# A new order for the opening of a linear-attention and gated-MLP kernel, with named PSUM banks and the first weight columns in four loads

## The chip, the cores and the metric

The kernel runs on one NeuronCore of one Trainium2 chip. The metric is the device time of one execution in microseconds (us). Before the change it is 321.68 us, the median of three runs (321.1 to 321.99). The profiled execution took 320.37 us, of which the profile's span covers 318.6 us.

The engines are named as in the profile: PE is the matrix engine (TensorE), PEld its weight loads, DVE is VectorE, ACT is ScalarE, POOL is GpSimd, SP is the engine that here only issues transfers. PSUM, which takes the matrix engine's results, has eight banks, numbered 0 to 7.

## The reference

Two steps in float32: a linear attention with a normalisation per head, then a gated MLP with a gated residual. Eight batches of 576 tokens, eight heads of 64, so 4608 tokens of 512 channels; the hidden width is 1536.

```python
kv  = einsum('bhsd,bhse->bhde', k, v)
o   = einsum('bhsd,bhde->bhse', q, kv)
x   = o / sqrt(mean(o * o, axis=-1) + 1e-6) * g_norm      # then (4608, 512)
g   = x @ w_gate
ffn = (0.5 * g * (1 + erf(g / sqrt(2))) * (x @ w_val)) @ w_out
out = x + ffn / (1 + exp(-(x @ w_res)))
```

## The kernel before

The tokens are worked in blocks of 512: of each batch the first 512 tokens are one block, in four tiles of 128 (`j`), and the 64 left over of all batches make a ninth block. Everything is computed in fp16 with fp32 sums. Block b's MLP runs on PE while the attention of batch b + 1 or b + 2 is worked beside it, so PE has work without a break, except in the opening: there batch 0 has no MLP beside it, and its attention must be through before the first MLP product.

The schedule is manual (`tc.manual_schedule()`, line 83): each engine executes its instructions in the order in which the program writes them. The opening's order is a string of words, `opening` (lines 1294 to 1299), read by `first_gval` and `f_piece`. A word names a step, then a pair of heads `pr` from 0 to 3 (128 channels), sometimes a half of the tiles (`a`, `b`), and in the last place an engine (`A`, `D`, `P`). An instruction that waits holds back what stands behind it on its own engine. For one pair the steps run as follows.

- `qc`, `kc`, `vc` cast the float32 arrivals of q, k and v to fp16. `lk` and `lv` put the last 64 tokens of k and v in place.
- `qT` transposes q on PE (four transposes), `qo` copies the result out of PSUM.
- `kv` multiplies k and v (six products), `kvo` (DVE) masks it into SBUF, `o` multiplies by q (four products).
- `sq` squares o (ACT), `rd` sums per head (DVE), `rt` is the root (ACT), `ri` the reciprocal (DVE), `t` the product o times reciprocal (DVE).
- `xT` transposes t (PE), and `xo` copies it out, scaled by the column `gcol` of g_norm.
- `g` and `v` are the products of that pair's 128 channels with the first 256 columns of w_gate and w_val, added up over the four pairs in four PSUM tiles (two of 128 columns for each weight).
- `warm` is a number of products of zeros, `keep_warm`, which nothing reads.

The first 256 columns of w_gate and w_val come as float32 through SP's queue, after all of q, k and v of batch 0 (line 1077), and are cast by the words `wcg` and `wcv` (half of the channels each). The other columns, `wg1` to `wg3` and `wv1` to `wv3` (256, 512 and 512 columns), are words too: POOL issues a transfer that casts on the way (`load_columns`, line 146). After the opening POOL issues in this order w_res (line 1600), batch 1 (`load_batch`, lines 120 to 122 and 109: q, k, v, then the last rows of k and of v), and w_out in four transfers (`load_wo`, line 1602: products 0 and 1, 2 and 3, 4 to 7, 8 to 11 of the hidden width).

PSUM tiles are taken from two rings of banks, `pmoe` and `pattn` (`Banks`, lines 61 to 75). A tile taken without a bank gets the ring's next one, so the bank follows from the order of the steps. A new tile in a bank must wait until the last reader of the tile before it is done.

After the opening come the MLP products of block 0: `m_gval(0, f)` for f from 2 to 7 (line 410, 8 products of 512 columns each), then a group of four by fewer products (line 946), the residual gate (line 430), the attention products of batch 1 (lines 187, 208), and then the products with w_out, one f after the other (line 447, `m_ffn`), with the second attention product of batch 1 (line 230) behind f = 0.

Of the kernel before, what the change touches and what calls it, by code (L numbers as in the profile page):

```python
# [8 lines left out]
FP32 = mybir.dt.float32  # L9
FP16 = mybir.dt.float16  # L10
# [8 lines left out]
def kernel(  # L19
# [15 lines left out]
    nc = tc.nc  # L35
    P = nc.NUM_PARTITIONS
    B, H, S, D = q.shape
    C = H * D
    F = moe_w_gate.shape[1]
    NP = H // 2  # L40
    NF = F // P
    NJ = 4
# [4 lines left out]
    WCS = (256, 256, 512, 512)  # L47
# [24 lines left out]
                self.turn.append(bank)  # L72
            return psum.tile(shape, dtype, tag=f"bank{bank}", name=name)

    pmoe, pattn = Banks(3, 1, 0, 2, opening=(0, 1, 2)), Banks(4, 5, 6, 7)

    def banks_behind():

# [55 lines left out]
    wg_c, wv_c = [], []  # L134
# [8 lines left out]
    th_all = finp.tile([P, NJ, C], FP32, bufs=1, name="th")  # L143
    res_all = finp.tile([P, NJ, C], FP32, bufs=1, name="osb")

    def load_columns(dst, src, i):
        c0 = sum(WCS[:i])
        nc.gpsimd.dma_start(out=dst[i], in_=src[:, c0 : c0 + WCS[i]].rearrange("(cc p) f -> p cc f", p=P))

    def load_wg(i):  # L150
        load_columns(wg_c, moe_w_gate, i)

    def load_wv(i):
        load_columns(wv_c, moe_w_val, i)

    def load_wo(f0, f1):
        nc.gpsimd.dma_start(
# [872 lines left out]
    for which in "kv":  # L1030
        if which == "k":
            t = hidp.tile([P, NF, NJ * P], FP16, tag="hid", name=which + "f").rearrange("p a b -> p (a b)")
        else:
            t = hid_s
# [8 lines left out]
    for which in "kv":  # L1043
        t = hid_of[which]
        rest = t[:, 2 * H * NJ * D :]
# [26 lines left out]
    w_raw = {}  # L1072
    for n, t in (("g", moe_w_gate), ("v", moe_w_val)):
        pool, tag = (stage, "qraw") if n == "g" else (qkvp, "k16")
        w_raw[n] = pool.tile([P, H, NJ * D], FP16, tag=tag, name=f"w{n}f")
        w_raw[n] = w_raw[n].rearrange("p a b -> p (a b)").bitcast(FP32).rearrange("p (c f) -> p c f", c=NP)
        nc.sync.dma_start(out=w_raw[n], in_=t[:, 0 : WCS[0]].rearrange("(cc p) f -> p cc f", p=P))
    ident32 = moep.tile([P, P], FP32, tag="ge", name="ident32")
    make_identity(nc, ident32)

# [10 lines left out]
    one32 = consts.tile([1, 1], FP32, name="one32")  # L1091
# [5 lines left out]
        out=of_head, in_=ident32.rearrange("p (r h) -> p h r", h=HH), op=ALU.add, axis=mybir.AxisListType.X  # L1097
    )
    grow32 = moep.tile([1, 2, D], FP32, tag="ge", name="grow32")
# [9 lines left out]
    def keep_warm(n):  # L1109
        for _ in range(n):  # L1110
            nc.tensor.matmul(idle, lhsT=zeros[:, 0:P], rhs=zeros, start=True, stop=True)  # L1111
# [5 lines left out]
    xT0, t0 = xT_t[0], t_t[0]  # L1117
    rms0 = consts.tile([P, NJ, H], FP32, name="rms0")
    rinv0 = consts.tile([P, NJ, H], FP32, name="rinv0")
    first = {}  # L1120
# [4 lines left out]
    def of_pair(pr):  # L1125
        return slice(2 * pr, 2 * pr + 2), slice(pr * P, (pr + 1) * P)

    def f_cast(which, pr, copy):
        hs, _ = of_pair(pr)
        dst, src = b16_t[0, which], raw[0, which]  # L1130
        if which == "v":
            copy(out=dst[:, hs, :], in_=src[:, hs, :])
        else:
            copy(
                out=dst.rearrange("p j h d -> p h j d")[:, hs, :, :],
                in_=src.rearrange("p h (j d) -> p h j d", j=NJ)[:, hs, :, :],
            )

    def f_k_last(half, engs):

        raw_ = first_raw[0][half].rearrange("p (j d) -> p j d", j=2)
        for j, eng in enumerate(engs):
            eng.tensor_tensor(
                out=first_last[0][:, j, half * HH : (half + 1) * HH, :],
                in0=raw_[:, j, None, :].to_broadcast([P, HH, D]),
                in1=of_head[:, :, None].to_broadcast([P, HH, D]),
                op=ALU.mult,
            )

    def f_v_last(half, copy):  # L1150
        raw_ = first_raw[1][half].rearrange("p (j d) -> p j d", j=2)
        copy(out=first_last[1][:, half], in_=raw_[:, :, None, :].to_broadcast([P, 2, 2, D]))

    def f_qT(pr):
        q16 = b16_t[0, "q"].rearrange("p j h d -> p j (h d)")
        first["qT", pr] = ps = pattn.tile([P, NJ, P], FP16, tag="at", name="qtp")
        for j in range(NJ):
            nc.tensor.transpose(ps[:, j, :], q16[:, j, of_pair(pr)[1]], ident)

# [2 lines left out]

    def f_kv(pr):

        first["kv", pr] = ps = pattn.tile([P, P], FP32, tag="at", name="kvp")
        k16 = b16_t[0, "k"].rearrange("p j h d -> p j (h d)")
        hs, cs = of_pair(pr)
        for j in range(NJ):
            nc.tensor.matmul(
                ps, lhsT=k16[:, j, cs], rhs=b16_t[0, "v"][:, hs, j * D : (j + 1) * D], start=(j == 0), stop=False  # L1170
            )
        for j in range(2):
            kl = first_last[0][:, j].rearrange("p h d -> p (h d)")[:, cs]
            vl = first_last[1][:, pr // 2, j].rearrange("p e d -> p (e d)")
            nc.tensor.matmul(ps, lhsT=kl, rhs=vl, start=False, stop=(j == 1))
# [2 lines left out]
        nc.vector.tensor_tensor(out=s0["kv2"][:, pr, :], in0=first["kv", pr], in1=mask, op=ALU.mult)  # L1178

    def f_o(pr):  # L1180
        pool, tag = (pmoe, "mm") if pr < 2 else (pattn, "at")
        first["o", pr] = ps = pool.tile([P, NJ, P], FP32, tag=tag, name="op")
        for j in range(NJ):
            nc.tensor.matmul(
                ps[:, j, :], lhsT=s0["qT"][:, j, pr, :], rhs=s0["kv2"][:, pr, :], start=True, stop=True
            )
# [27 lines left out]
        )  # L1214

    def f_xT(pr, j0, j1):
        first["xT", pr, j0] = ps = pattn.tile([P, j1 - j0, P], FP16, tag="at", name="xtp")
        for j in range(j0, j1):
            nc.tensor.transpose(ps[:, j - j0, :], t0[:, j, of_pair(pr)[1]], ident)

# [22 lines left out]
    def f_piece(word):  # L1243

        name = word.rstrip("0123abADP")
        rest = word[len(name) :]
        pr = int(rest[0])
        j0, j1 = {"a": (0, NJ // 2), "b": (NJ // 2, NJ)}.get(rest[1:2], (0, NJ))
        eng = rest[-1:]
        if name in ("qc", "kc", "vc"):  # L1250
            f_cast(name[0], pr, engines[eng])
        elif name == "lk":
            f_k_last(pr, (nc.gpsimd if eng == "P" else nc.vector, nc.vector))
        elif name == "lv":
            f_v_last(pr, engines[eng])
        elif name == "warm":
            keep_warm(pr)
        elif name == "wg":
            load_wg(pr)
        elif name == "wv":  # L1260
            load_wv(pr)
        elif name in ("wcg", "wcv"):
            cs = slice(2 * pr, 2 * pr + 2)
            engines[eng](out=(wg_c if name == "wcg" else wv_c)[0][:, cs, :], in_=w_raw[name[-1]][:, cs, :])
        elif name == "qo":
            f_qT_out(pr, engines[eng])
        elif name in ("qT", "kv", "kvo", "o", "rt", "ri"):
            {"qT": f_qT, "kv": f_kv, "kvo": f_kv_out, "o": f_o, "rt": f_sqrt, "ri": f_rinv}[name](pr)
        elif name in ("sq", "rd", "t", "xT"):
            {"sq": f_sq, "rd": f_red, "t": f_t, "xT": f_xT}[name](pr, j0, j1)  # L1270
        elif name == "xo":
            f_xT_out(pr, j0, j1, eng)
        elif name == "g":
            f_mm(wg_c, 0, pr, j0, j1)
        elif name == "v":
            f_mm(wv_c, 1, pr, j0, j1)
# [1 line left out]
    keep_warm(5)  # L1278

    gcol = consts.tile([P, 1], FP32, name="gcol")  # L1280
    gcp = pattn.tile([P, 1], FP32, tag="at", name="gcp")
    nc.tensor.matmul(gcp, lhsT=grow32.rearrange("p h d -> p (h d)"), rhs=one32, start=True, stop=True)
    nc.vector.tensor_copy(out=gcol, in_=gcp)
    g16 = consts.tile([P, C], FP16, name="g16")
    gps = pattn.tile([P, C], FP32, tag="at", name="gbp")
    nc.tensor.matmul(gps, lhsT=ones16, rhs=grow16.rearrange("p h d -> p (h d)"), start=True, stop=True)
    nc.vector.tensor_copy(out=g16, in_=gps)

    keep_warm(3)

    opening = """
    qc1P qc0A qT1 qT0 kc1P kc0A qo0D warm3 lk0D lv0P qo1A warm3 vc1D vc0A kv1 qc2A kv0 kvo1 kvo0 o1 kc2P qT2
    lk1P sq1 qo2D o0 warm3 warm2 vc2P sq0 lv1A rd1 kv2 qc3P rt1 kvo2 rd0 kc3A qT3 wg1 wv1 ri1 o2 rt0 t1 warm3 warm1 sq2 vc3D
    rd2 qo3A xT1 kv3 wg2 wcg0P rt2 kvo3 ri0 ri2 warm2 o3 t2 xo1A wcg1P sq3a wcv0P sq3b g1 xT2 rd3a wcv1P rd3b
    wv2 t0 rt3 xo2A wg3 wv3 v1 xT0 ri3 xo0A g2 v2 t3a t3b xT3a xT3b g0 xo3aA xo3bD gelu v0 g3a v3a g3b v3b
    """

    def first_gval(ahead):
        hids[0] = hidp.tile([P, NF, NJ * P], FP16, tag="hid", name="hid")
        for word in opening.split():
            if word == "gelu":
                nc.scalar.preload_act_table_set("gelu_and_others")
            else:
                f_piece(word)
        for f in ahead:
            f()
        for f in range(2):  # L1310
            m_act(0, f, tiles[f, 0][0], tiles[f, 1][0])
# [153 lines left out]
    for blk in GROUPS:  # L1465
        t = token_sums(blk, nc.vector)
# [50 lines left out]
    for blk in range(B + 1):  # L1517
# [21 lines left out]
        else:  # L1539
            slots = [lambda f=f: m_gval(blk, f) for f in range(NF)]  # L1540
            groups = GROUPS.get(blk, ())
            if groups:
                n = NF - GF * len(groups)
# [93 lines left out]
```

## Time and profile before

| What | us |
|---|---|
| median of three runs | 321.68 |
| profiled execution | 320.37 |
| its span | 318.6 |
| PE busy in the span | 310.8 |
| DVE, ACT, POOL busy | 274.6, 210.4, 186.9 |
| first product of the opening (zeros) | 1.17 |
| first product of the words g and v | 15.80 |
| first product of line 410, right behind the opening | 20.73 |
| first product with w_out, line 447 | 42.41 |

All times inside the execution are counted from the start of the span. PE is busy 98% of it. Its idle time on waits for other engines lies in the first 18 us. From 20.73 on the answer on waits lists none on PE, and the chain of work that ended last runs through PE's products; each of them starts when the one before is through. What the opening needs is paced by the transfers of q, k and v, which land between 4.6 and 13.1 us, and of the first weight columns, which land at 14.5 (w_gate) and 16.0 us (w_val).

### The profile page before, as it was taken

To read this page: it belongs to the slowest core of one execution; us is meant where nothing else is said; L and a number is where in the kernel's file an instruction comes from. 1 tells how busy PE (TensorE), PEld (TensorE's weight loads), DVE (VectorE), ACT (ScalarE), POOL (GpSimd) and SP (SyncE) were. 2 spreads that over 40 slices of the span, in tenths; PEclk is the share of its full clock that TensorE was granted. 3 is DMA by queue.
4 is the path that set the end of the run, shared out by engine and by line. 5 is a ranking of instruction groups with operands and counts; after the bars stand their busy time and mean duration, and the time that the engine had idled before them with its cause. 6 is when DMAs were issued, how large, how long until landed. Compare 5 with 4: busy or idle time off the path is not lost.

```text
span 318.6 us, 7756 instructions
## 1 busy us (share of the span) xinstructions
PE 310.8 (98%) x3044; PEld 247.1 (78%) x3044; DVE 274.6 (86%) x486; ACT 210.4 (66%) x385; POOL 186.9 (59%) x249
## 2 busy tenths in 40 slices
PE   8999999999999999999999999999999999999993
PEld 3544755444788888888888888888888888888882
DVE  5788889799898999989998999899988777897774
ACT  3773685465848794889487958795767467836760
POOL 2792351573769479756975687417751375396332
PEclk9999999999999999999999999999999999999998
DMA  7999999799994898579947995700340003001204
GB/s 250 330 204 205 194 206 192 173 174 160 173 110 94 188 156 80 98 201 139 96 82 217 122 112 84 215 5 0 69 148 2 0 3 135 0 2 52 82 2 132
DMA packets 76694, 38.90 MB, mean 122 GB/s; under 512 B 42098, under 2 KB 74354, under 8 KB 76658
## 3 DMA queue, kind: packets, MB, share of 16 engines
q0 software_dynamic: 38752, 17.17, 42.5%
q1 hardware_dynamic: 37328, 20.71, 25.5%
q8 instruction: 24, 0.39, 0.5%
q10 hardware_dynamic: 578, 0.52, 0.5%
q14 instruction: 12, 0.10, 0.1%
HBM read 38.80 MB, written 9.44 MB: 151 GB/s over the span
## 4 chain that ended last, share of the span: by engine, by line
PE 96%; DVE 3%; issue 0%; DVEq 0%
PE Ag L946 12%; PE Av L946 12%; PE wA L515 12%; PE Fv L946 6%; PE Fg L946 6%; PE gps L410 5%; PE vps L410 5%; PE rA L566 4%; PE fps L447 3%; PE Ev L946 3%; PE Eg L946 3%; PE wF L515 3%; PE wE L515 3%; PE wD L515 3%; PE w L515 2%; PE idle L1111 2%
## 5 line engine op out<-in xcount | busy, mean ns | idle before, releaser
L983 POOL TENSOR_TENSOR hid<-ge,c 128x512 f16<-128x512 f16 x22 | 25.6, 1162 | 38.8 <-ACT ge L977 38.8
L515 PEld LDWEIGHTS <-hid_s 128*128 128x128 f16 x384 | 37.6, 98 | 4.3
L946 PEld LDWEIGHTS <-wsv 128*128 128x128 f16 x352 | 34.1, 98 | 4.8 <-issue 0.7
L946 PEld LDWEIGHTS <-wsg 128*128 128x128 f16 x352 | 34.3, 98 | 4.0
L361 POOL TENSOR_TENSOR t<-t,g 128x512 f16<-128x512 f16 x32 | 37.0, 1187 | 0.0
L702 POOL TENSOR_TENSOR osb<-osb,t 128x512 f32<-128x512 f32 x28 | 34.1, 1244 | 0.0
L956 ACT COPY Eg<-Ag 128x512 f32<-128x512 f32 x22 | 12.8, 582 | 27.7 <-PE Ag L946 27.7
L515 PEld LDWEIGHTS <-hid 128*128 128x128 f16 x288 | 28.2, 98 | 3.5
L946 PEld LDWEIGHTS <-wg 128*128 128x128 f16 x264 | 25.8, 98 | 3.2
L946 PEld LDWEIGHTS <-wv 128*128 128x128 f16 x264 | 25.8, 98 | 3.0
L946 PE MATMUL Ag<-ts,wsg 128*128 128x256 f16 x176 | 26.4, 273 | 0.0
L946 PE MATMUL Av<-ts,wsv 128*128 128x256 f16 x176 | 26.4, 273 | 0.0
L967 DVE TENSOR_TENSOR Fg<-Ag,d 128x512 f32<-128x512 f32 x22 | 15.3, 696 | 11.3 <-ACT d L960 7.6
L258 DVE TENSOR_REDUCE ss<-sq 128x8 f32<-128x512 f32 x32 | 20.5, 678 | 1.7 <-ACT sq L253 1.7
L398 ACT ACTIVATE ge<-gps 128x512 f16<-128x512 f32 x20 | 11.7, 597 | 14.3 <-PE gps L410 14.2
L515 PE MATMUL wA<-wo_ts,hid_s 128*128 128x256 f16 x168 | 20.6, 273 | 0.0
L977 ACT ACTIVATE ge<-Eg 128x512 f16<-128x512 f32 x22 | 13.1, 597 | 10.4 <-PE Eg L946 10.4
L977 ACT ACTIVATE ge<-c 128x512 f16<-128x512 f32 x22 | 13.8, 625 | 7.7 <-DVE c L967 7.7
L345 DVE TENSOR_TENSOR t<-op,ny 128x512 f16<-128x512 f32 x28 | 18.4, 682 | 0.5 <-POOL ny L319 0.4
L967 DVE TENSOR_TENSOR c<-Ag,d 128x512 f32<-128x512 f32 x22 | 15.1, 689 | 4.1 <-PE Ag L946 4.1
L977 ACT ACTIVATE ge<-Fg 128x512 f16<-128x512 f32 x22 | 13.0, 590 | 8.4 <-PE Fg L946 6.3
L410 PE MATMUL gps<-xT,wg 128*128 128x512 f16 x72 | 18.5, 379 | 0.0
(219 smaller groups left out, 857.9 us busy)
## 6 DMA issues: line engine op xcount, KB each, us to landing
out_dram<-osb SPq DMA_DIRECT2D x14, 512.0 KB, 3.7
qraw<-in_q_dram POOLq DMA_DIRECT2D x7, 512.0 KB, 6.6
k<-in_k_dram POOLq DMA_DIRECT2D x7, 512.0 KB, 8.7
v<-in_v_dram POOLq DMA_DIRECT2D x7, 512.0 KB, 10.8
wg<-in_moe_w_gate_dram POOLq DMA_DIRECT2D x2, 512.0 KB, 8.3
wv<-in_moe_w_val_dram POOLq DMA_DIRECT2D x2, 512.0 KB, 8.8
wo<-in_moe_w_out_dram POOLq DMA_DIRECT2D x2, 512.0 KB, 14.3
out_dram<-osb SPq DMA_DIRECT2D x4, 256.0 KB, 4.5
```

Of the source, the lines that this page charges most:

```text
L258: nc.vector.tensor_reduce(out=out_, in_=sqs.pop((b, i)), op=ALU.add, axis=mybir.AxisListType.X)
L345: nc.vector.tensor_tensor(out=t, in0=o, in1=scale, op=ALU.mult)
L361: eng.tensor_tensor(out=t_t[blk][:, jj, :], in0=t_t[blk][:, jj, :], in1=g16, op=ALU.mult)
L410: nc.tensor.matmul(ps[:, j0 * P : j1 * P], lhsT=w[:, cc, :], rhs=xT_t[blk][:, j0:j1, cc, :], start=(cc == 0 and j0 == 0), stop=(cc == NP - ...
L515: nc.tensor.matmul(ps[:, e - es[0], :], lhsT=a[:, f, e * P : (e + 1) * P], rhs=b[:, f, :], start=(start and e == es[0] and f == 0), stop=( ...
L566: nc.tensor.matmul(out_[:, e, :], lhsT=x_[:, e, cc, :], rhs=w_[:, cc, :], start=(first and e == 0 and cc == 0), stop=(cc == 1), skip_group ...
L702: nc.gpsimd.tensor_tensor(out=res_all[of], in0=res_all[of], in1=t_t[blk][of], op=ALU.add)
L946: nc.tensor.matmul(out_[:, r, :], lhsT=lhsT, rhs=rhs, start=(first and r == 0 and c == 0), stop=(c == 1), skip_group_check=True,)
L956: nc.scalar.copy(out=tile_of("E", u), in_=ps["A", u])
L967: nc.vector.tensor_tensor(out=dst, in0=ps["A", u], in1=sb["d", u], op=ALU.add)
L977: nc.scalar.activation(out=ge[q], in_=source(q, "g"), func=AF.Gelu)
L983: eng.tensor_tensor(out=dst, in0=ge[q], in1=source(q, "v"), op=ALU.mult)
```

## The change

The words of `opening` stand in another order, and some name another engine. Every PSUM tile of the opening's attention steps gets a bank by name (`BANK`). The first 256 columns of w_gate and w_val come in four transfers instead of two: channels 0 to 255 of w_gate, of w_val, then channels 256 to 511 of each. The columns `wv2` come in two transfers of 256 columns (`wv2a`, `wv2b`). The product and the copy that make `gcol` move from ahead of the opening into it, behind the first cast of v, and the copy of `g16` goes from DVE to ACT. There are 20 products of zeros instead of 25.

```diff
-    pmoe, pattn = Banks(3, 1, 0, 2, opening=(0, 1, 2)), Banks(4, 5, 6, 7)
+    pmoe, pattn = Banks(3, 1, 0, 2, opening=(0,)), Banks(4, 5, 6, 7)
...
-    def load_columns(dst, src, i):
+    def load_columns(dst, src, i, part):
+        lo, hi = (part * WCS[i] // 2, (part + 1) * WCS[i] // 2) if part is not None else (0, WCS[i])
         c0 = sum(WCS[:i])
-        nc.gpsimd.dma_start(out=dst[i], in_=src[:, c0 : c0 + WCS[i]].rearrange("(cc p) f -> p cc f", p=P))
+        nc.gpsimd.dma_start(
+            out=dst[i][:, :, lo:hi], in_=src[:, c0 + lo : c0 + hi].rearrange("(cc p) f -> p cc f", p=P)
+        )
...
-        nc.sync.dma_start(out=w_raw[n], in_=t[:, 0 : WCS[0]].rearrange("(cc p) f -> p cc f", p=P))
+    for cs in (slice(0, NP // 2), slice(NP // 2, NP)):
+        for n, t in (("g", moe_w_gate), ("v", moe_w_val)):
+            nc.sync.dma_start(
+                out=w_raw[n][:, cs, :], in_=t[:, 0 : WCS[0]].rearrange("(cc p) f -> p cc f", p=P)[:, cs, :]
+            )
...
+    BANK = {"qT": (6, 4, 7, 7), "kv": (7, 5, 6, 4), "o": (2, 1, 6, 4), "xT": (7, 5, 7, 4), "xTb": (0, 0, 0, 5)}
...
-        first["qT", pr] = ps = pattn.tile([P, NJ, P], FP16, tag="at", name="qtp")
+        first["qT", pr] = ps = pattn.tile([P, NJ, P], FP16, name="qtp", bank=BANK["qT"][pr])
...
-        pool, tag = (pmoe, "mm") if pr < 2 else (pattn, "at")
-        first["o", pr] = ps = pool.tile([P, NJ, P], FP32, tag=tag, name="op")
+        first["o", pr] = ps = pattn.tile([P, NJ, P], FP32, name="op", bank=BANK["o"][pr])
...
-    gcp = pattn.tile([P, 1], FP32, tag="at", name="gcp")
-    nc.tensor.matmul(gcp, lhsT=grow32.rearrange("p h d -> p (h d)"), rhs=one32, start=True, stop=True)
-    nc.vector.tensor_copy(out=gcol, in_=gcp)
     g16 = consts.tile([P, C], FP16, name="g16")
-    gps = pattn.tile([P, C], FP32, tag="at", name="gbp")
+    gps = pattn.tile([P, C], FP32, name="gbp", bank=5)
     nc.tensor.matmul(gps, lhsT=ones16, rhs=grow16.rearrange("p h d -> p (h d)"), start=True, stop=True)
-    nc.vector.tensor_copy(out=g16, in_=gps)
-
-    keep_warm(3)
+    def g_column():
+        gcp = pmoe.tile([P, 1], FP32, name="gcp", bank=3)
+        nc.tensor.matmul(gcp, lhsT=grow32.rearrange("p h d -> p (h d)"), rhs=one32, start=True, stop=True)
+        nc.vector.tensor_copy(out=gcol, in_=gcp)
+
+    keep_warm(4)
 
     opening = """
-    qc1P qc0A qT1 qT0 kc1P kc0A qo0D warm3 lk0D lv0P qo1A warm3 vc1D vc0A kv1 qc2A kv0 kvo1 kvo0 o1 kc2P qT2
-    lk1P sq1 qo2D o0 warm3 warm2 vc2P sq0 lv1A rd1 kv2 qc3P rt1 kvo2 rd0 kc3A qT3 wg1 wv1 ri1 o2 rt0 t1 warm3 warm1 sq2 vc3D
-    rd2 qo3A xT1 kv3 wg2 wcg0P rt2 kvo3 ri0 ri2 warm2 o3 t2 xo1A wcg1P sq3a wcv0P sq3b g1 xT2 rd3a wcv1P rd3b
-    wv2 t0 rt3 xo2A wg3 wv3 v1 xT0 ri3 xo0A g2 v2 t3a t3b xT3a xT3b g0 xo3aA xo3bD gelu v0 g3a v3a g3b v3b
+    qc0A qc1D g16 qT1 qT0 kc0A kc1D lk0P qo1A qo0D lv0P warm3 vc1D gcol vc0P kv1 qc2A kv0 kvo1 o1 kvo0 kc2P qT2 o0
+    lk1D sq1 lv1P warm3 sq0 rd1 vc2P rd0 rt1 kv2 qc3P qo2A warm2 ri1 kvo2 rt0 wg1 t1 kc3A o2 qT3 sq2 ri0 xT1 warm2 vc3P t0
+    qo3A wv1 rd2 kv3 wcg0A xT0 warm1 kvo3 rt2 xo1D wcv0P o3 xo0A ri2 g1 t2 wg2 sq3b v1 sq3a rd3b wcg1A xT2 wv2a rd3a g0 xo2D
+    rt3 v0 wv2b wcv1A ri3 g2 t3b wg3 t3a xT3b v2 xo3bD xT3a wv3 g3b xo3aD gelu v3b g3a v3a
     """
+    pattn.turn = [6, 7, 5, 4]
...
+            if word == "g16":
+                nc.scalar.copy(out=g16, in_=gps)
+            elif word == "gcol":
+                g_column()
```

The tiles of `kv` and `xT` take their banks from `BANK` in the same way, and `f_piece` passes the half of the columns on to `load_wg` and `load_wv`. Nothing behind the opening is edited.

More of the change, by code (lines that the diff above doesn't have):

```diff
@@ L144, with load_wg, load_wv @@
     res_all = finp.tile([P, NJ, C], FP32, bufs=1, name="osb")
-    def load_columns(dst, src, i):
+    def load_columns(dst, src, i, part):
+        lo, hi = (part * WCS[i] // 2, (part + 1) * WCS[i] // 2) if part is not None else (0, WCS[i])
         c0 = sum(WCS[:i])
-        nc.gpsimd.dma_start(out=dst[i], in_=src[:, c0 : c0 + WCS[i]].rearrange("(cc p) f -> p cc f", p=P))
[L150 to L154, printed above, removed]
+        nc.gpsimd.dma_start(
+            out=dst[i][:, :, lo:hi], in_=src[:, c0 + lo : c0 + hi].rearrange("(cc p) f -> p cc f", p=P)
+        )
+    def load_wg(i, part=None):
+        load_columns(wg_c, moe_w_gate, i, part)
+    def load_wv(i, part=None):
+        load_columns(wv_c, moe_w_val, i, part)
     def load_wo(f0, f1):
@@ L1163, in f_kv @@
     def f_kv(pr):
-        first["kv", pr] = ps = pattn.tile([P, P], FP32, tag="at", name="kvp")
+        first["kv", pr] = ps = pattn.tile([P, P], FP32, name="kvp", bank=BANK["kv"][pr])
         k16 = b16_t[0, "k"].rearrange("p j h d -> p j (h d)")
@@ L1216, in f_xT @@
     def f_xT(pr, j0, j1):
-        first["xT", pr, j0] = ps = pattn.tile([P, j1 - j0, P], FP16, tag="at", name="xtp")
+        bank = BANK["xTb" if j0 else "xT"][pr]
+        first["xT", pr, j0] = ps = pattn.tile([P, j1 - j0, P], FP16, name="xtp", bank=bank)
         for j in range(j0, j1):
@@ L1257, in f_piece @@
             keep_warm(pr)
[L1258 to L1261, printed above, removed]
+        elif name in ("wg", "wv"):
+            (load_wg if name == "wg" else load_wv)(pr, {"a": 0, "b": 1}.get(rest[1:2]))
         elif name in ("wcg", "wcv"):
@@ L1303, in first_gval @@
         for word in opening.split():
-            if word == "gelu":
+            if word == "g16":
+                nc.scalar.copy(out=g16, in_=gps)
+            elif word == "gcol":
+                g_column()
+            elif word == "gelu":
                 nc.scalar.preload_act_table_set("gelu_and_others")
```

## The prediction

> **What bounds the kernel now.** I read the page's slices first, then the matrix engine's own timeline of the first 45 us, then the waits of PE, then every transfer by itself. The page:
>
> ```profile
> span 318.6 us, 7756 instructions
> PE   8999999999999999999999999999999999999993
> DMA  7999999799994898579947995700340003001204
> GB/s 250 330 204 205 194 206 192 173 174 160 173 110 94 188 156 80 98 201 139 96 82 217 122 112 84 215 5 0 69 148 2 0 3 135 0 2 52 82 2 132
> ```
>
> A slice is 7.97 us. PE is full from the second on, and the transfers are full for the first six. PE's timeline (start, length, instruction, idle time before it):
>
> ```profile
> 1.17 2.31 PE L1111 MATMUL idle<-zeros 128*128 128x512 f16 x5 [1.17 <-DVE zeros L1082]
> 6.49 2.71 PE L1111 MATMUL idle<-zeros 128*128 128x512 f16 x6
> 9.04 0.39 PE L1169 MATMUL kvp<-v,k 128*128 128x128 f16 x4
> ...
> 15.80 0.59 PE L1235 MATMUL gps<-xT,wg 128*128 128x512 f16 x2 [0.24 <-POOL wg L1264]
> 16.78 0.39 PE L1235 MATMUL vps<-xT,wv 128*128 128x512 f16 x1 [0.16 <-POOL wv L1264]
> 17.47 0.38 PE L1235 MATMUL vps<-xT,wv 128*128 128x512 f16 x1 [0.31 <-DVE t L1209]
> 20.73 1.03 PE L410 MATMUL gps<-xT,wg 128*128 128x512 f16 x4
> ...
> 42.27 0.20 PE L208 MATMUL kvp<-vl,kl 128*64 128x64 f16 x2
> 42.41 1.04 PE L447 MATMUL fps<-wo,hid 128*128 128x512 f16 x4
> ```
>
> The opening ends at 20.73. Behind it PE has no break, so a shorter opening seems worth what it saves. But the products with w_out at 42.41 need a transfer. POOL's timeline, and then the answer on transfers for the stretch of that single issue (last number: us from issue to landing):
>
> ```profile
> 24.51 0.69 POOL L109 DMA_DIRECT2D vl<-in_v_dram  x1 [0.99 <-DMA wv<-in_moe_w_val_dram]
> 27.03 0.71 POOL L157 DMA_DIRECT2D wo<-in_moe_w_out_dram  x1 [1.84 <-DMA wg<-in_moe_w_gate_dram]
> ```
>
> ```profile
> wo<-in_moe_w_out_dram POOLq DMA_DIRECT2D x1, 256.0 KB, 15.3
> ```
>
> 27.03 + 15.3 = 42.33: the first part of w_out lands 0.08 us before PE uses it. The same sum for the others, landing against use: wv2 24.22 against 25.05; v of batch 1 40.59 against 41.65; its last rows (vl) 24.51 + 16.6 = 41.11 against 41.79; w_out's second part 43.64 against 44.82, third 46.19 against 46.55, fourth 49.29 against 50.01. So the true state is: PE full, and the transfers level with it at 42.4.
>
> **What the Trainium skill says.** "DMA: Bandwidth & Descriptors", "Issuing engines are not separate DMA queues": transfers of all issuing engines end up on the same 16 engines. The trace agrees: POOL's first packet moves at about 14.8, when SP's run out (14.5 to 15: 166 packets of SP's queue, 8 of POOL's), although POOL issued at 12.14; from 3 us to past 50 no half microsecond is free. "TensorE: Matmul & The Clock Gate", Part 1: the array runs at half clock until a free-running window of about 3.4 us has been busy. Here a product of zeros takes 0.427 us until 9.04 and 0.216 later. "PSUM — Partial Sum Buffer", "PSUM bank collisions raise a hardware error": two engines must not touch one bank together, so a named bank can bring a wait. The trace has one: v's second tile at 17.47 waited 0.31 for the `t` that still read its bank.
>
> **The change part by part.** Steps are from one engine's start to the next; from the last PE product to a reader of its PSUM I count 0.20 (kv's end 9.37 to `kvo` 9.57), from a writer to PE 0.05.
>
> *Ahead of the first kv.* The zeros end at 3.31, gbp (0.43) at 3.85, then four zeros (1.71): 5.56. The q casts, on ACT and DVE, end at 5.24. Eight transposes of 0.107: 6.42. Three zeros instead of six: 7.70; gcp follows (two passes, 0.45). v lands at 8.03, its DVE cast (0.42) ends 8.50, so kv1 starts at 8.55, not 9.04. Gain 0.5. DVE does `gcol` (0.16) where it waits for kv anyway; g16 on ACT (about 0.58, as ACT's copy of qT) lies between casts that wait for transfers.
>
> *Pairs 0 to 2.* These wait for landings that the diff doesn't touch. v of pair 2 lands at 10.78: POOL's cast 0.61, kv2 at 11.55 (11.66 before), `kvo` to 12.37. Only DVE's order gains: `t1` runs 12.36 to 13.05 (13.23 to 13.92 before), `t0` 13.12 to 13.81 (16.74 before), which also takes away the bank wait of 0.31.
>
> *Pair 3 and the weights.* v of pair 3 lands at 13.07. POOL's cast ends 13.70, kv3 0.33 and 0.20, `kvo` to 14.61, o3 to 14.88 (15.40). The four loads carry the bytes of two, 0.73 us each at the rate of before (w_gate landed 1.46 behind v): about 13.8, 14.5, 15.3, 16.0. Half of v's weights can be cast from 14.5 instead of 16.0; POOL's cast ends 15.25 (16.72). xo1 on DVE takes 0.35 to 0.62 (a 512-wide `tensor_scalar` from SBUF 0.34; 256 wide from PSUM 0.35, which may double); I take 0.62: 14.60 to 15.20. So g1 starts at 15.25, v1 at 15.68.
>
> *To the end.* PE has eight times 0.43 for g and v and three times 0.22 of transposes: 4.1, so 19.35 without a break. DVE behind 15.29: t2 0.61, two sums 0.68, xo2 0.55, ri3 0.15, two halves of t3 0.68, then transposes and copies; the last xo3 ends at 18.95, and g3a and v3a follow to 19.44. ACT's three casts of weights (0.53 each) end at 17.5, its gelu table load (1.28) at 18.7. I take 19.44: the opening is 1.3 us shorter. With xo at 0.35 it is 19.2.
>
> *What then comes too late.* Everything from 20.73 moves up by 1.3, the transfers do not. Bytes and order in POOL's queue are the same, and the queue can't start earlier, since SP's packets end when they did. wg1 (17.24), wv1 (18.5) and wg2 (21.66) are in time for 19.4, 20.3 and 22.9. wv2 whole at 24.22 would be too late for 23.75; its first half lands some 1.3 earlier. wg3 (26.76) delays DVE's sums by about 1 us, PE's users have 1.8. Then v and vl hold PE from 40.35 to 41.2, and w_out's first part holds it until 42.33. A gain of 1.3 shrinks to 0.08.
>
> *What is added.* wv2 in halves writes 512-byte rows instead of 1 KB. Transfers with such rows landed 2.64 apart (w_res to q), with 1 KB rows 2.54 (wv2 to wg3): +0.12 (taken; between 0 and 0.26, the latter from w_res to v, 2.92 each). POOL's extra issue (0.77) hides in the queue: from vl on each issue waits for the eighth transfer before it, in the new order too. SP's two extra issues (0.37 each) have nothing behind them.
>
> Sum: −0.08 + 0.12, rounded up for the wait: +0.1 us, so 320.5 against the profiled 320.37. The median lies 1.3 above that execution: **321.8 us, no change.**
>
> **The rivals.**
>
> *The gain passes.* −1.3 us, 320.4. For it: nothing in PE's waits names w_out. Against it: 42.33 is a landing, and no edit moves it. It needs a part of the transfers that isn't packed; PE's instruction fetches, one in 16 to 20 us and one in 36 to 40, stretch two landings by 0.6 (wg2) and 0.8 (v), and might fall elsewhere.
>
> *Slower: POOL starves its own queue.* wg2 is issued behind POOL's cast `wcv0`, at 15.25 instead of 13.86. From issue to first packet an idle queue took about 1.7 (142.78 to some 144.5). wg1 and wv1 last until 14.9 + 2 × 1.3 = 17.5. So there are 0.55 us of room; from an issue at 15.8 on every microsecond is a hole in a full queue and moves w_out by as much. If `wcv0` has to wait for both halves of w_val (16.0), wg2 goes at 16.65: a hole of 0.85, and 0.1 from above, 322.7. Against it: the q casts of batch 0 started at 4.65 on the first of three loads of one tile.
>
> *The clock stays low.* PE rests from about 8.15 to 8.55, and a window could miss. At half clock until 12.45 the kv steps cost 0.6, which the waiting at w_out hides. Until 19.25 (9.04 plus three windows) the opening ends at about 21.2, +0.5: 322.2.
>
> That the change doesn't do what it says: the named banks of o, g and v are those that the rings gave; what is new lies in `t0`'s place.
>
> **How the numbers follow.** Forecast 0.60; the gain passes 0.19; starved queue 0.14; clock 0.07. A measurement here tells 0.3% (0.97 us) from no change. The first rival is faster, but for a part that stays under the bound; the starved queue is slower in two of three cases; the forecast strays over either bound in a few of a hundred, by spread between runs (0.9 us over three). Faster 0.20, within 0.58, slower 0.22. The range holds the first rival's 320.4 and the starved queue's 322.7 with a little spread: 320.2 to 323.0. The forecast's own range is 321.3 to 322.3.
>
> **What would show it.** Right: the first product of line 410 near 19.4; PE waits of some 0.8 us at line 208 and of more than 1 us in all ahead of line 447; line 447 again at 42.4 to 42.6; SP's last weight load at 16.0. Wrong: line 447 near 41.1, or w_out's landing more than 0.5 us from 42.4. kv1 taking over 0.6 us shows the low clock; no POOL packets around 17.5 the hole.

## The result and the profile after

| | Before | After |
|---|---|---|
| median, six runs each on one chip | 321.38 us | 321.38 us |
| lowest of the six | 320.96 | 320.68 |
| profiled execution | 320.37 | 322.43 |
| its span | 318.6 | 319.6 |
| first product right behind the opening | 20.73 | 19.41 |
| first product with w_out | 42.41 | 43.53 |

The ratio after to before is 0.9999, with a 95% interval of 0.9977 to 1.0021: no change, as forecast (321.8). One of the six executions of after fell into a slower state (329.88 us), as did the profiled one of a variant below (330.08), and both are left out of the ratios. The opening did become shorter, and the time did not. The profiled execution of after took 1.0 us more than its median; of its 322.43 us, 2.8 lie outside the span, where before had 1.8. In the code after, line 410 has become 413, 447 is 450, 208 is 211, 946 is 949 and 430 is 433.

The page of after, its first lines and the slices for PE and the transfers:

```profile
span 319.6 us, 7753 instructions
PE   7899989999999999999999999999999999999993
DMA  7999999799994699479947694800340003000204
```

Before had nines on PE from the second slice to the last but one. Now the second slice (8 to 16 us) is at 8, as is the sixth (40 to 48). The transfers are as full in the first six slices as they were. Where PE stands still is in the answer on waits for PE, us in total, times, longest:

```profile
PE kvp L1178 <- DVE gcol L1295: 1.5, 1, 1.5
PE idle L1118 <- DVE zeros L1089: 1.2, 1, 1.2
PE fps L450 <- DMA wo<-in_moe_w_out_dram: 0.6, 1, 0.6
PE kvp L1178 <- POOL v L1139: 0.4, 1, 0.4
PE vps L413 <- DMA wv<-in_moe_w_val_dram: 0.3, 1, 0.3
PE kvp L211 <- DMA vl<-in_v_dram: 0.3, 1, 0.3
```

Three waits on a transfer (w_out, wv2a, the last rows of v) are new; in before PE waited for no transfer. They stand at these places of PE's timeline (start, length, instruction, and in brackets the idle time before it with what ended it):

```profile
5.90 0.81 PE L1118 MATMUL idle<-zeros 128*128 128x512 f16 x3
...
8.54 0.40 PE L1178 MATMUL kvp<-v,k 128*128 128x128 f16 x4 [1.52 <-DVE gcol L1295]
...
19.41 1.03 PE L413 MATMUL gps<-xT,wg 128*128 128x512 f16 x4
...
24.41 1.04 PE L413 MATMUL vps<-xT,wv 128*128 128x512 f16 x4 [0.28 <-DMA wv<-in_moe_w_val_dram]
...
42.21 0.22 PE L211 MATMUL kvp<-vl,kl 128*64 128x64 f16 x2 [0.28 <-DMA vl<-in_v_dram]
...
43.53 1.04 PE L450 MATMUL fps<-wo,hid 128*128 128x512 f16 x4 [0.63 <-DMA wo<-in_moe_w_out_dram]
```

Set beside before, line by line, the gain goes as follows. At 19.41 PE is 1.32 us ahead. The v product of f = 4 starts at 24.41 instead of 25.05: 0.64 ahead. The first product of line 433 starts at 37.18, in before's line 430 at 37.21: 0.03 ahead. The first product with w_out is 1.12 behind. The chain that ended last, in order of time, now runs through the transfers themselves:

```profile
17.32 10.96 DMA wg<-in_moe_w_gate_dram
...
28.57 14.92 DMA wo<-in_moe_w_out_dram
```

The chain of before stood on PE's products here. In after, 17.32 is POOL's issue of wg3, and 28.57 is the issue of w_out's first part, which waits for the eighth transfer before it (wg3). 28.57 + 14.92 = 43.49: PE starts 0.04 later. So this landing set the end here, and it came 1.1 later than the 42.4 on which the forecast rests.

### The profile page after: what moved, and what is told of

It is laid out like the page before. It is cut to its first block, busy times and chain, and to the rows that moved or that the text cites. A ratio compares the mean times of both kernels' runs of the same rounds, so it can differ in the third digit from the quotient of the medians.

```text
span 319.6 us, 7753 instructions
## 1 busy us (share of the span) xinstructions
PE 309.5 (97%) x3039; PEld 245.6 (77%) x3039; DVE 275.2 (86%) x488; ACT 210.8 (66%) x385; POOL 188.0 (59%) x248
## 4 chain that ended last, share of the span: by engine, by line
PE 84%; DMA 11%; SPq 1%; POOL 1%; DVE 1%; issue 0%; DVEq 0%
PE Ag L949 12%; PE Av L949 11%; PE wA L518 11%; PE Fv L949 6%; PE Fg L949 6%; DMA wg<-in_moe_w_gate_dram 5%; DMA wo<-in_moe_w_out_dram 5%; PE rA L569 4%; PE gps L413 3%; PE fps L450 3%; PE vps L413 3%; PE Ev L949 3%; PE Eg L949 3%; PE wD L518 3%; PE wF L518 3%; PE wE L518 3%
## 5 line engine op out<-in xcount | busy, mean ns | idle before, releaser
L401 ACT ACTIVATE ge<-gps 128x512 f16<-128x512 f32 x20 | 11.9, 598 | 15.6 <-PE gps L413 13.6
L413 PE MATMUL vps<-xT,wv 128*128 128x512 f16 x72 | 18.5, 379 | 0.4 <-DMA wv<-in_moe_w_val_dram 0.3
```

The costliest lines, as they stand in the source:

```text
L413: nc.tensor.matmul(ps[:, j0 * P : j1 * P], lhsT=w[:, cc, :], rhs=xT_t[blk][:, j0:j1, cc, :], start=(cc == 0 and j0 == 0), stop=(cc == NP - ...
```

## The experiments

Two theories to begin with. Theory 1 is the forecast's: up to w_out's first part the transfers are as long as PE's work, and a shorter opening changes only where PE stands still. The rival: the new order itself costs on PE or DVE, behind the opening, what it saves in it, and the transfers are only the name on the wait. Each ratio is to 43 or 55 executions of before on the same chip, with medians of 320.77 us (fewer bytes, pads in the opening), 320.56 (pads behind it, two loads, cast loads) and 321.07 (the rest).

**Fewer bytes, in both kernels.** The transfers wg1 and wv1 are left out, their tiles are set to a constant, and the later words move up into their places (shown in the changed kernel; in before the words move in the same way):

```diff
+    nc.gpsimd.memset(wg_c[1], 0.01)
+    nc.gpsimd.memset(wv_c[1], 0.01)
...
-    lk1D sq1 lv1P warm3 sq0 rd1 vc2P rd0 rt1 kv2 qc3P qo2A warm2 ri1 kvo2 rt0 wg1 t1 kc3A o2 qT3 sq2 ri0 xT1 warm2 vc3P t0
-    qo3A wv1 rd2 kv3 wcg0A xT0 warm1 kvo3 rt2 xo1D wcv0P o3 xo0A ri2 g1 t2 wg2 sq3b v1 sq3a rd3b wcg1A xT2 wv2a rd3a g0 xo2D
-    rt3 v0 wv2b wcv1A ri3 g2 t3b wg3 t3a xT3b v2 xo3bD xT3a wv3 g3b xo3aD gelu v3b g3a v3a
+    lk1D sq1 lv1P warm3 sq0 rd1 vc2P rd0 rt1 kv2 qc3P qo2A warm2 ri1 kvo2 rt0 wg2 t1 kc3A o2 qT3 sq2 ri0 xT1 warm2 vc3P t0
+    qo3A wv2a rd2 kv3 wcg0A xT0 warm1 kvo3 rt2 xo1D wcv0P o3 xo0A ri2 g1 t2 wv2b sq3b v1 sq3a rd3b wcg1A xT2 wg3 rd3a g0 xo2D
+    rt3 v0 wv3 wcv1A ri3 g2 t3b t3a xT3b v2 xo3bD xT3a g3b xo3aD gelu v3b g3a v3a
```

In the kernel before:

> The kernel before without the two transfers of columns 256 to 511 of w_gate and w_val (their tiles are filled with a constant early on, so these columns' products are left out of the result's meaning, not out of the work); 0.5 MB of writes less, so all that stands behind in POOL's queue lands about 2.5 us earlier. Theory 1 (the transfers up to w_out's first part set the end): PE of the kernel before waited for none of them, so no change, -0.1 to 0.1 us. Rival (the shorter opening is lost in the order of the engines, transfers play no part): no change as well.

In the changed kernel:

> The changed kernel, the same two transfers left out in the same way. Theory 1: with the transfers out of the way the 1.3 us that the opening saves come through, -1.0 to -1.3 us against the kernel before (ratio 0.996 to 0.997), and PE waits for no w_out transfer. Rival: still equal to the kernel before, within 0.3 us.

Measured: before without the two transfers 320.99 us, ratio to before 0.9996 [0.998, 1.0012]; after without them 319.28 us, ratio 0.9952 [0.9933, 0.9972], somewhat more than was expected. The fastest executions differ by what the opening saves: 320.22 in before, 320.34 in before without the transfers, 318.92 in after without them. With the transfers in place the fastest of after (320.19, of 22 below) is only 0.1 under the fastest of before on that chip (320.28). PE's timeline of the changed kernel without the two transfers:

```profile
19.73 1.03 PE L413 MATMUL gps<-xT,wg 128*128 128x512 f16 x4
...
41.40 1.04 PE L450 MATMUL fps<-wo,hid 128*128 128x512 f16 x4
```

and of the kernel before without them:

```profile
21.33 1.03 PE L410 MATMUL gps<-xT,wg 128*128 128x512 f16 x4
...
43.00 1.04 PE L447 MATMUL fps<-wo,hid 128*128 128x512 f16 x4
```

Neither w_out line has a bracket, so nothing was waited for. From the end of the opening to w_out PE took 21.67 us in both; the unchanged kernel before has 42.41 − 20.73 = 21.68. That is PE's own time for this stretch, in the new order as in the old: the new order costs nothing behind the opening once the bytes are out of the way, and before, with its full transfers, was already at this floor. The rival falls. (Both openings end later than without the edit, by 0.6 us in before and 0.3 in after. The two constants are through on POOL at 3.1 us, ahead of its first cast, so they need not be the reason: in before the first products of kv took 0.63 us for four instead of 0.39, as they did in a variant without constants, the one with the pad behind the opening below, and in after q, k and v landed some 0.3 late.)

**A delay of known length, first inside the opening.** Five products of zeros (1.08 us at the 0.216 of each) ahead of the word `g1`:

```diff
-    ... sq3a wcv0P sq3b g1 xT2 rd3a wcv1P rd3b
+    ... sq3a wcv0P sq3b warm3 warm2 g1 xT2 rd3a wcv1P rd3b
```

> The kernel before with five more products of zeros (1.08 us) on PE ahead of the word g1. Theory 1: PE has no room, w_out's first part landed 0.08 us before its use, so the full 0.8 to 1.1 us (ratio 1.0025 to 1.0035). Rival (transfers play no part): the same 1.1 us.

The same in the changed kernel, ahead of its `g1`:

> The changed kernel with the same five products of zeros ahead of g1. Theory 1: PE waits for transfers later anyway, so the 1.1 us vanish: 0 to +0.3 us against the changed kernel, and so against the kernel before. Rival: +1.1 us (ratio 1.0034).

Measured: before with the pad 320.62 us, ratio 0.9989 [0.9977, 1.0], a miss; after with the pad 320.53 us, ratio 0.999 [0.9975, 1.0005]. The trace tells why the first is no test: its opening ended at 20.78 instead of 20.73. PE does not set the opening's end at `g1`; the pad filled time in which PE would have stood later. It reached w_out at 42.85 and waited 0.34 us there, so in this execution before, too, was held by the landing. In the changed kernel the pad moved the end by 0.76, and the time did not follow. So the delay had to go where nothing can absorb it.

**The same delay right behind the opening.** In `m_gval`, ahead of the first product of line 410 (413):

```diff
+        if blk == 0 and f == 2:
+            for _ in range(5):
+                nc.tensor.matmul(gps, lhsT=ident, rhs=g16, start=True, stop=True)
```

> The kernel before with five more products of 512 columns (1.08 us) on PE at the head of the product f = 2 of block 0, right behind the opening, so that all of PE's later work is shifted. Theory 1 (w_out's first part is level with PE in the kernel before, so that only the executions where it lands late have room): +0.5 to +1.0 us (ratio 1.0015 to 1.003). Rival (transfers play no part): +1.08 us.

> The changed kernel with the same five products in the same place. Theory 1: the room of 1.2 us ahead of w_out's first part takes them up, 0 to +0.3 us against the kernel before (ratio up to 1.001). Rival: +1.08 us (ratio 1.0034).

PE's timeline of before with the pad (the first line is the pad itself):

```profile
21.11 1.24 PE L424 MATMUL gps<-g,ident 128*128 128x512 f16 x5
22.19 1.03 PE L410 MATMUL gps<-xT,wg 128*128 128x512 f16 x4
...
43.85 1.04 PE L450 MATMUL fps<-wo,hid 128*128 128x512 f16 x4
```

and of after with it:

```profile
19.43 1.24 PE L427 MATMUL gps<-g,ident 128*128 128x512 f16 x5
20.51 1.03 PE L413 MATMUL gps<-xT,wg 128*128 128x512 f16 x4
...
42.48 1.04 PE L453 MATMUL fps<-wo,hid 128*128 128x512 f16 x4 [0.23 <-DMA wo<-in_moe_w_out_dram]
```

In before the delay of 1.08 us costs 1.0 (321.55 against 320.56; ratio 1.0036 [1.0021, 1.005]): PE walks from 22.19 to 43.85 in 21.66 us and never waits. By itself this does not tell the theories apart: 1.0 is the upper end of theory 1, and close to the rival's 1.08. The changed kernel does. In after it costs nothing (320.42; ratio 0.9986 [0.9967, 1.0004]): PE still stands 0.23 us for w_out. This is the plainest showing of theory 1: the changed kernel carries over a microsecond of slack on PE that the transfers eat.

**One part undone: the first weight columns in two loads again.**

```diff
-    for cs in (slice(0, NP // 2), slice(NP // 2, NP)):
-        for n, t in (("g", moe_w_gate), ("v", moe_w_val)):
-            nc.sync.dma_start(
-                out=w_raw[n][:, cs, :], in_=t[:, 0 : WCS[0]].rearrange("(cc p) f -> p cc f", p=P)[:, cs, :]
-            )
+        nc.sync.dma_start(out=w_raw[n], in_=t[:, 0 : WCS[0]].rearrange("(cc p) f -> p cc f", p=P))
```

> The changed kernel with the first columns of w_gate and w_val in two loads again, as in the kernel before. POOL's cast of the first half of w_val then waits for the whole load (16.0 us instead of 14.5), and POOL's transfers wg2, wv2a and so on are issued 1.5 us later. Theory of the starved queue: a hole of about 0.8 us in POOL's packets near 17.5, w_out's first part 0.8 us later, +0.6 to +0.9 us (ratio 1.002 to 1.003). Rival (enough is queued): no hole, no change, though the opening ends about 1 us later.

Measured: 321.69 us, ratio 1.0049 [1.003, 1.0068]. The profiled execution of this kernel took 330.08 us; it has a wait of 6 us at 288 us that no other has, but the granted clock is 1.00 up to 46 us, and only that stretch is read here. PE's and then POOL's timeline:

```profile
20.57 1.03 PE L413 MATMUL gps<-xT,wg 128*128 128x512 f16 x4
...
43.37 1.04 PE L450 MATMUL fps<-wo,hid 128*128 128x512 f16 x4 [0.50 <-DMA wo<-in_moe_w_out_dram]
```

```profile
16.22 0.62 POOL L1268 CAST wv<-wvf 128x512 f16<-128x512 f32 x1 [1.65 <-DMA wvf<-in_moe_w_val_dram]
16.77 0.75 POOL L149 DMA_DIRECT2D wg<-in_moe_w_gate_dram  x1
```

and the rate of all transfers from 12 to 21 us, in 40 slices of 0.225 us (GB/s):

```profile
GB/s 346 350 360 346 341 350 346 360 328 360 341 360 346 280 232 205 198 203 198 182 178 175 196 203 193 205 84 27 32 77 64 55 164 164 164 196 209 191 200 209
```

The same answer of the changed kernel as it is:

```profile
GB/s 355 350 351 351 346 346 355 346 346 341 346 355 328 262 232 212 196 198 196 178 168 178 196 187 189 260 187 162 164 180 198 196 187 189 184 184 173 205 189 193
```

The high rates at the left are SP's float32 transfers, those around 195 POOL's casting ones. With two loads POOL's cast of w_val waits 1.65 us for the whole of w_val, wg2 is issued behind it at 16.77 instead of 15.11, and POOL's queue runs dry: six slices from 17.85 to 19.2 us at 56 GB/s on average. At 195 to 200 GB/s that is (1 − 56/197) × 1.35 = 0.97 us of transfer lost. This is the prediction's rival of the starved queue, at nearly its case (an issue at 16.65, a hole of 0.85, 322.7 us); the measured cost is 1.1 us by the medians (321.69 against 320.56) and 1.6 by the ratio. That PE is not what costs it is shown: the opening ends at 20.57, no later than in before, and PE stands 0.50 us for w_out. That each later landing moves by the hole is not shown. In this one execution wg2 and wg3 landed at 22.2 and 27.5, as they did without a hole in the changed kernel's second profile (22.4 and 27.5, below), and only v of batch 1 and w_out came later.

**The other part alone: four loads in the kernel before.**

```diff
-        nc.sync.dma_start(out=w_raw[n], in_=t[:, 0 : WCS[0]].rearrange("(cc p) f -> p cc f", p=P))
+    for cs in (slice(0, NP // 2), slice(NP // 2, NP)):
+        for n, t in (("g", moe_w_gate), ("v", moe_w_val)):
+            nc.sync.dma_start(
+                out=w_raw[n][:, cs, :], in_=t[:, 0 : WCS[0]].rearrange("(cc p) f -> p cc f", p=P)[:, cs, :]
+            )
```

> The kernel before with only the loads of the first weight columns changed to four (both weights' first two pairs of channels, then the others); the order of words stays. Theory 1: POOL's second cast of w_gate waits until 15.3, the casts of w_val end at about 17.1 as before, POOL's order of issues is untouched, so the opening ends at 20.5 to 20.9 and line 447 stands at 42.2 to 42.6: ratio 0.999 to 1.001. Rival (the loads are what shortens the opening): opening ends at 20.2 or earlier.

Measured: 321.0 us, ratio 1.0005 [0.9988, 1.0021]; the opening ended at 20.88, w_out's first product stood at 42.55. The loads alone shorten nothing, and the new order with two loads ended its opening at 20.57: it takes both to reach 19.41. The loads are what the new order needs so that POOL's cast does not hold back wg2.

**Would fewer bytes in SP's queue help?** The first columns come through POOL's queue, cast on the way (issued at 8.89 and 11.05), so that SP's four loads and four casts drop out:

```diff
-        nc.sync.dma_start(out=w_raw[n], ...)
...
-        elif name in ("wcg", "wcv"):
-            cs = slice(2 * pr, 2 * pr + 2)
-            engines[eng](out=(wg_c if name == "wcg" else wv_c)[0][:, cs, :], in_=w_raw[name[-1]][:, cs, :])
...
-    qc0A qc1D g16 qT1 qT0 kc0A kc1D lk0P qo1A qo0D lv0P warm3 vc1D gcol vc0P kv1 qc2A kv0 kvo1 o1 kvo0 kc2P qT2 o0
-    lk1D sq1 lv1P warm3 sq0 rd1 vc2P ...
+    qc0A qc1D g16 qT1 qT0 kc0A kc1D lk0P qo1A qo0D lv0P warm3 vc1D gcol vc0P wg0 kv1 qc2A kv0 kvo1 o1 kvo0 kc2P qT2 o0
+    lk1D sq1 lv1P wv0 warm3 sq0 vc2A ...
```

> The changed kernel, but the first columns of w_gate and w_val come through POOL's queue in two transfers that cast on the way, instead of four float32 loads on SP's queue and four casts; POOL's cast of v of pair 2 goes to ACT. Theory 1: what counts is how long the 16 engines are busy up to w_out's first part; SP's float32 loads run at 348 GB/s read, POOL's casting ones at about 395 to 408, so 1.05 MB takes about 0.35 us less, and the time falls by 0.3 to 0.4 us against the kernel before (ratio 0.9988 to 0.999) even if the opening gets no shorter. Rival (the opening's end decides): the time follows the opening's end.

Measured: 321.75 us, ratio 1.0043 [1.0026, 1.006], slower by 0.4%, against what both theories expected: the opening ended at 19.73, only 0.3 us later than in after. The rate from 12 to 21 us, in the same slices as above:

```profile
GB/s 264 232 196 200 196 193 175 198 168 209 177 162 132 130 157 150 166 175 164 134 141 155 166 168 178 175 187 187 150 162 198 178 275 191 164 168 200 171 189 196
```

POOL's queue starts earlier, but from 14.5 to 17.4 us it moves some 154 GB/s, where the changed kernel's, from 15.6 to 19, moves some 189, and w_out's first part lands at 43.48. That is not one late execution: eleven of the twelve have spans of 319.6 us or more, where the median of before on that chip is 318.7. Why the rate falls is not settled. POOL issues almost without a break from 13.66 on, but so it does in the changed kernel from 15.11 to 20.4, so that alone does not explain it; ACT took over a cast of v, which was not tried by itself.

**One term of the sum: wv2 in one transfer.** The words `wv2a` and `wv2b` become one `wv2`:

```diff
-    ... g1 t2 wg2 sq3b v1 sq3a rd3b wcg1A xT2 wv2a rd3a g0 xo2D
-    rt3 v0 wv2b wcv1A ri3 g2 ...
+    ... g1 t2 wg2 sq3b v1 sq3a rd3b wcg1A xT2 wv2 rd3a g0 xo2D
+    rt3 v0 wcv1A ri3 g2 ...
```

> The changed kernel with the columns wv2 in one transfer again (1 KB rows, one issue less on POOL). Theory 1 (transfers and PE level at w_out, so bytes and rate decide): the whole of wv2 is not there when its first 256 columns are wanted, so PE waits 0.3 to 1.2 us at f = 4, but w_out's first part lands where it did or 0.1 to 0.2 earlier, and the first product of line 450 stands within 0.3 us of where that landing puts it; the time is within 0.3% of the changed kernel, ratio to the kernel before 0.998 to 1.001. Rival (the 512-byte rows and the extra issue cost what hides the gain): line 450 0.5 us or more earlier, ratio 0.997 or less. Rival (PE's order decides, waits add up): +0.5 to +1 us, ratio 1.002 to 1.004.

And the changed kernel once more on the same chip:

> The changed kernel as it is, a second look at the same chip as its variants. Theory 1: the opening ends at 19.3 to 19.5 again; w_out's first part lands between 42.1 and 43.5, since this landing moves by more than a microsecond from one execution to the next, and the first product of line 450 follows it by less than 0.1 us; ratio 0.998 to 1.001. Rival (the late landings of the first profile belong to the order itself): landing again at 43.3 or later, ratio 1.001 to 1.003.

Measured: with one wv2 320.89 us, ratio 0.9997 [0.9978, 1.0016]; the changed kernel again 321.12 us, ratio 1.0004 [0.9986, 1.0022]. PE's timeline with one wv2:

```profile
24.45 1.04 PE L413 MATMUL vps<-xT,wv 128*128 128x512 f16 x4 [0.60 <-DVE wsg L481]
...
42.25 1.04 PE L450 MATMUL fps<-wo,hid 128*128 128x512 f16 x4 [0.26 <-DMA wo<-in_moe_w_out_dram]
```

and of the changed kernel's second profile:

```profile
19.44 1.03 PE L413 MATMUL gps<-xT,wg 128*128 128x512 f16 x4
...
42.77 1.04 PE L450 MATMUL fps<-wo,hid 128*128 128x512 f16 x4 [0.52 <-DMA wo<-in_moe_w_out_dram]
```

With one wv2 PE stands at f = 4 until 24.45: wv2, issued at 15.83, lands at 24.43. The named releaser, a sum on DVE, ends at 24.45 too, but the product does not need it: in the second profile of the changed kernel the same product starts at 23.76, ahead of these sums (23.78). The wait changes nothing, since w_out still ends later. The second profile has w_out's first part landing at 42.71, not at 43.47, and its chain says where the difference arises:

```profile
17.38 10.15 DMA wg<-in_moe_w_gate_dram
...
27.81 14.92 DMA wo<-in_moe_w_out_dram
```

w_out's first part takes 14.92 us from its issue in both profiles. Its issue comes 0.76 later in the first, because wg3 lands later, and wg2 already did (23.0 against 22.4). What held the transfers up there is open. That it belongs to the order is unlikely: on the chip of the second profile 7 of 22 executions of the changed kernel have spans of 319.6 us (the first profile's) or more, and 16 of 43 of before; the medians are 319.0 and 319.2.

**All profiles in one table.** First product with w_out, and the span, both from the profile of each run but the one with two loads. A landing is the issue and the answer's time to landing, which has one decimal, so it is good to some 0.05 us:

| Kernel | w_out landed | first product | span | span − product |
|---|---|---|---|---|
| before | 42.33 | 42.41 | 318.6 | 276.2 |
| before, four loads | 42.11 | 42.55 | 318.6 | 276.1 |
| before, pad in the opening | 42.76 | 42.85 | 319.0 | 276.2 |
| before, pad behind it | 42.51 | 43.85 | 320.0 | 276.2 |
| before, fewer bytes | 39.57 | 43.00 | 319.1 | 276.1 |
| after | 43.47 | 43.53 | 319.6 | 276.1 |
| after, again | 42.71 | 42.77 | 318.8 | 276.0 |
| after, pad in the opening | 42.12 | 42.17 | 318.3 | 276.1 |
| after, pad behind it | 42.41 | 42.48 | 318.5 | 276.0 |
| after, one wv2 | 42.24 | 42.25 | 319.0 | 276.8 |
| after, cast loads | 43.48 | 43.48 | 319.8 | 276.3 |
| after, fewer bytes | 39.51 | 41.40 | 317.4 | 276.0 |

From the first product with w_out on, ten of twelve profiles take 276.0 to 276.2 us (with one wv2, 0.6 more, in one execution, not followed up). So each of these spans is decided at that product. In every variant of after but the one with fewer bytes it follows the landing by less than 0.1 us; in before it follows PE's own work or the landing, whichever is later.

## Why the prediction was right

*What bounds the kernel: right.* The forecast read 42.33 against 42.41 as "PE full, and the transfers level with it". Fewer bytes and the pad behind the opening show both halves of it. Of the gain that the transfers hold back, 0.08 was forecast to pass; of the fastest executions on one chip, 0.1 us of it does (320.19 against 320.28).

*Ahead of the first kv: the time right, the way there not.* kv1 starts at 8.54 (8.55 forecast), kept by v's landing and cast. But the zeros ran at 0.22 us each from 5.9 on, not at 0.43 until gcp, and so ended at 6.6 instead of 7.70. "TensorE: Matmul & The Clock Gate", Part 1, of the Trainium skill lets the clock rise after a busy window that is free-running, that is, not tied to the start of the kernel. The runs agree: the moment moves between executions of the same words. In the second profile of after the same three zeros start at 6.49, not at 5.90. In before, the first kv stands at 9.04; in the variant with the pad ahead of `g1` it stands at 8.51, at full rate, and in the one with fewer bytes at 9.05, at half rate (four products in 0.63 us), although PE's words up to there are those of before. So the earlier rise here can be the execution's own, and shows nothing of the order. PE then rests 1.5 us (put down to `gcol` here, and to DVE's cast of v in the second profile), and the rival of the low clock did not come: kv1's four products take 0.40 and the next four 0.38, against 0.39 in before.

*The opening's steps: right within 0.15.* kv2 at 11.58 (11.55), the end of o3 at 15.01 (14.88), g1 at 15.18 (15.25), v1 at 15.61 (15.68), end at 19.41 (19.44). xo1 on DVE took 0.47, between the two bounds, where 0.62 was taken. The landing of SP's last weight load, forecast for 16.0, is not in the trace.

*What then comes too late: the mechanism right, its places off.* The forecast had PE wait 0.8 us at v's last rows and until 42.4 at w_out. In the two profiles of after the waits there are 0.28 and 0.39 at v's last rows, 0.63 and 0.52 at w_out; in the second that is 0.91 in all, where more than 1 us was the sign. The first half of wv2, forecast 1.3 ahead of 24.22, landed at 24.4 and 23.7, and PE waited 0.28 for it in the first profile. One step failed by its size: the delay of DVE's sums by wg3, which should have left PE alone ("PE's users have 1.8"). DVE's timeline of the second profile:

```profile
27.55 0.42 DVE L481 TENSOR_TENSOR wsg<-wg 128x512 f16<-128x512 f16 x1 [1.96 <-DMA wg<-in_moe_w_gate_dram]
...
28.35 0.68 DVE L402 TENSOR_TENSOR hid<-ge,vps 128x512 f16<-128x512 f16 x1
...
31.94 0.42 DVE L481 TENSOR_TENSOR wsv<-wv,wsv 128x512 f16<-128x512 f16 x1
```

and PE's:

```profile
28.08 1.03 PE L413 MATMUL gps<-xT,wg 128*128 128x512 f16 x4
29.08 1.02 PE L413 MATMUL vps<-xT,wv 128*128 128x512 f16 x4
...
31.69 0.60 PE L949 MATMUL Ag<-ts,wsg 128*128 128x256 f16 x4
32.40 0.60 PE L949 MATMUL Av<-ts,wsv 128*128 128x256 f16 x4
```

wg3 lands at 27.5, and the first sum over its columns starts at 27.55; in before it started at 26.79, so DVE is 0.76 late here while PE is 1.29 ahead. The v product at 29.08 starts 1.00 after the g product instead of 0.86: `hid`, which reads a v product out of PSUM, stood behind the sums and ended at 29.03. The product at 32.40 starts 0.71 after the one before it instead of 0.44: the last sum ended at 32.36. The gaps too short for the answer on waits add up: PE's lead of 1.29 at 19.44 is 0.80 when line 433 begins (36.41 against 37.21). That DVE would hand its delay on was not in the forecast. The loss hides behind w_out's landing, as the rest does.

*The landing: not as sure as it was written.* 42.45 was forecast, from one execution, and more than 0.5 us off was to count as wrong. The first profile of after has 43.47, over that bound; the second profile, the two padded kernels and the one with one wv2 have 42.12 to 42.71. The working took a number that moves by over a microsecond between executions for a constant. That the medians agree to 0.0 us is in part luck: the interval of the ratio is 1.4 us wide.

*What is added: not to be told.* The 0.12 for wv2 in halves is smaller than what landings vary by: from wg2's landing to wg3's it took 5.1 us in before and with one wv2, 5.2 and 5.3 in the two profiles of after, from landings known to 0.1. The working of the term is not clear either: the gaps that it names (2.64 and 2.92 less 2.54) give 0.10 and 0.38, not 0.12 and 0.26.

*The rivals.* The gain passes, but only when bytes are taken out (319.28). The starved queue is real, and the four loads keep the kernel from it: with two, wg2 is issued 1.66 us later (16.77 against 15.11) and the queue runs dry.

## What to carry to other kernels

A stretch in which one engine is full can be held by a second resource that arrives just in time and shows no wait at all. Before work is taken out of it, set every landing beside its first use: the smallest of these margins bounds what a shorter engine can gain, and one profile does not give it to better than the landings vary, here over a microsecond. When an order is changed, look at what POOL's own work puts ahead of its issues, since a queue that runs dry loses what it could have moved: here a hole worth 0.97 us stood beside 1.1 us of time.

## What the runs showed that was not expected

- The landing of w_out's first part moves between executions of one and the same kernel (43.47 and 42.71), with the transfers issued in the same order. The difference is there from wg2's landing on (23.0 and 22.4); the cause is open.
- POOL's casting queue moved some 154 GB/s for about 3 us, instead of some 189, when it was started earlier (cast loads). The cause is open.
- What lies outside the span is under 2.0 us in all 204 executions of before and its variants on record, and 2.0 to 3.4 in 21 of 117 of the changed kernel and its variants. So the time of one execution can be a microsecond longer with nothing of it in the span, which is as much as the effect that was looked for, and it was seen with the new order alone. In the 22 executions of the changed kernel again it is 1.98 us on average, against 1.81 in before beside it. The cause is open.
